# Thirty small loads on SP's queue, and 384 skipped products at the head of TensorE's program, in a decode kernel that streams a key and value cache

## The chip, the cores and the metric

One core of one Trainium2 chip runs the whole kernel. The metric is the time of one execution on the device, in microseconds (us); the figure for a kernel is the median of several runs.

## The reference, cut to what matters

One decode step for two batch entries. A token vector `x` (2 x 512) is normalised, projected to 32 query heads, and attends over a cache of 32,768 keys and values for each of 8 key/value heads. A small two-layer network on the same normalised vector gives a gate.

```python
xn = _layernorm(A_x)
q  = (xn @ wq)                                   # 512 x 4096
scores = einsum("bhqd,bhkd->bhqk", q, k) * 128**-0.5
o  = einsum("bhqk,bhkd->bhqd", softmax(scores), v)
s  = o.reshape(2, 1, 4096) @ wo                  # 4096 x 512
h  = relu(xn @ w1 + b1) ** 2
g  = silu(h @ w2 + b2)
out = A_x + s * g
```

The caches are `k_cache` and `v_cache`, each 2 x 8 x 32768 x 128 in float32. They make up almost all of the bytes that are read.

## The kernel before, in words

**Tiles.** There are 16 steps, one for each pair of batch entry and key/value head. The keys of a step come in two loads (`load_k`) of 128 partitions x 16,384 numbers into `kring`, which has three slots of 64 rows; its values come in two loads of the same size (`load_v`) into `vbuf`. Each such load is 8.4 MB. VectorE transposes the keys in blocks (`dve_keys`, L309), TensorE makes scores from them (`te_scores`, L270) and weights the values (`te_values`, L280), ScalarE evicts and exponentiates.

**Order of the loads.** All large loads are issued by SP through the helper `load` (L84), one after another, in the order in which the program writes them. A load into `kring` waits for VectorE's transposes of what stood there (`transposed`); a load into `vbuf` waits for TensorE's products with the values that stood there (`PV`). While SP waits for one mark, everything behind it on its queue waits too. ACT issues four small loads at the start and the store of the result at the end.

**Start.** SP issues the query weights `wq` into `vbuf` (L138), then the first keys (L139) and one half load of the next (L140). `wq_in` releases the projection products (L210), whose result is turned into `qT` by copies and transposes (L227 to L235). The first instructions of TensorE are four transposes of the normalised vector (L200); they wait for VectorE.

**Middle.** From the second step on, PE, ScalarE and VectorE each run a hardware loop (L442 to L489), whose outermost PE loop is placed at slot 0 of a block of its code (`head_slot`, L442). SP's loads are written out (L495 to L502).

**End.** The last two value loads go into `kring` and `vbuf` (L507, L508), then the output weights `wo` in five pieces (L515 to L519). The last products are L525 and L533; `spare` (L538 to L540) adds products whose result nobody reads. The result leaves by ACT's store (L587).

Of the kernel before, what the change touches and what calls it, by code (L numbers as in the profile page):

```python
# [5 lines left out]
F32 = mybir.dt.float32  # L6
# [5 lines left out]
P = 128  # L12
# [40 lines left out]
def gqa_decode_kernel(nc, x, kc, vc, wq, wo, w1, b1, w2, b2, out):  # L53
    B, _, D = x.shape
    _, HKV, SK, DH = kc.shape
# [15 lines left out]
    def sb(name, *shape):  # L71
        return nc.alloc_sbuf_tensor(name, (P,) + shape, F32).ap()

    def bank(name, n=1):
        t = nc.alloc_psum_tensor(name, (P, n * 512), F32).ap()
        return t if n == 1 else t.rearrange("p (n f) -> p n f", n=n)

    SP, ACT, DVE, POOL, TE = (Lane(nc, e, n) for e, n in (
        (nc.sync, "sp"), (nc.scalar, "act"), (nc.vector, "dve"), (nc.gpsimd, "pool"), (nc.tensor, "pe")))
    tensor, vector, scalar, gpsimd, sync = nc.tensor, nc.vector, nc.scalar, nc.gpsimd, nc.sync  # L80

    def load(lane, dst, src, sem, *marks):
        lane.wait(*marks)
        return sem.after(lane.eng.dma_start(dst, src))  # L84

    def dma(name):
        return Count(nc, name, 16)
# [9 lines left out]
    def k_rows(m):  # L97
        s, u = divmod(m, 2)
        return rows(kc, s).rearrange("(p u r) d -> p u r d", p=P, u=2)[:, u]
# [20 lines left out]
    def transposed(q):  # L120
        return KT[1].at(q + 1)

    def load_k_half(m, i, *marks):
        c = k_order(m)[i][1]
        return load(SP, k_slot(2 * m + i), k_rows(m)[:, c * SLOT:(c + 1) * SLOT], k_sems[m % 2], *marks)

    def load_k(m):
        a = m % 2
        return load(SP, kring[:, a * SLOT:(a + 2) * SLOT, :], k_rows(m), k_sems[a], transposed(max(2 * m - 2, -1)))
# [6 lines left out]
    wo_t = [kflat[:, a * SLOT * DH:a * SLOT * DH + 16 * D].rearrange("p (r e) -> p r e", r=16) for a in (2, 0)]  # L136

    wq_in = load(SP, wq_t, wq.rearrange("(p d) f -> p d f", p=P), dma("wq"))  # L138
    k0_in = load_k(0)  # L139
    load_k_half(1, 1)  # L140

# [8 lines left out]
    ident = sb("ident", P)  # L150
# [21 lines left out]
    mx_ps, fin_ps, pj_ps, acc_ps = bank("mx_ps"), bank("fin_ps"), bank("pj_ps"), bank("acc_ps")  # L172
# [22 lines left out]
    t = DVE(lambda: vector.reciprocal(st[:, 3:4], st[:, 2:3]), t)  # L195
    t = DVE(lambda: vector.tensor_scalar(xn, xn, st[:, 3:4], None, op0=ALU.mult), t)
    xnT = sb("xnT", ND, 32)
    TE.wait(t, have_ident)
    for d in range(ND):
        t = TE(lambda: tensor.transpose(mx_ps[:, d * P:(d + 1) * P], xn.rearrange("p (k d) -> p d k", d=ND)[:, d], ident))  # L200
# [22 lines left out]
    for f in range(2):  # L223
        for h in range(REP):
# [8 lines left out]
            v = t_ps.rearrange("p (e g y) -> p g e y", e=4, g=NG)  # L233
# [10 lines left out]
    def set_q(s):  # L244
        hkv, b = divmod(s, B)
        return POOL(lambda: gpsimd.tensor_tensor(
            qz.rearrange("p e (x h) -> p e x h", h=REP),
            qT[:, b, hkv].rearrange("p h e -> p e h")[:, :, None, :].to_broadcast([P, 4, 8, REP]),
            bm[:, None, :, None].to_broadcast([P, 4, 8, REP]), op=ALU.mult),
            *((have_qT, have_bm) if s == 0 else (PA[1].at(4 * s + 1),)), on=QZ if s else None)  # L250
# [125 lines left out]
    for d in range(ND):  # L376
        for g in range(NG):
            t = TE(lambda: tensor.matmul(pj_ps[32 * g:32 * g + 32, :FG], xnT[:, d, :], w1_t[:, d, g * FG:(g + 1) * FG],
                                         start=False, stop=(d == ND - 1)))
# [37 lines left out]
    for j in range(4):  # L417
        t = TE(lambda: tensor.matmul(fin_ps[32 * j:32 * j + 32, 0:P], ones[0:1, 0:32], b2t[:, j * P:(j + 1) * P],
                                     start=False, stop=True, skip_group_check=True))
# [12 lines left out]
    act_probs(0, have_p)  # L432


    def registers(eng, **values):
        for name, v in values.items():
            r = eng.alloc_register(name)
            eng.reg_mov(r, v)
            yield r

    rq, rv, rs = registers(tensor, rq=5, rv=16, rs=1)
    with nc.Fori(1, NS, 1, engines=[PE], head_slot={PE: 0}):  # L442
        with nc.Fori(0, 2, 1, engines=[PE]):
# [13 lines left out]
        tensor.reg_add(rs, rs, 1)  # L457

    aq, av, as_ = registers(scalar, aq=6, av=1, as_=1)
    with nc.Fori(1, NS, 1, engines=[AE]):  # L460
        for u in range(2):
# [10 lines left out]

    seen = Count(nc, "seen").sem
    dq, dk, ds = registers(vector, dq=5, dk=48, ds=1)
    with nc.Fori(1, NS, 1, engines=[VE]):
        for q in range(4):
# [18 lines left out]
    for s in range(1, NS):  # L495
# [5 lines left out]
        if s + 1 < NS:  # L501
            set_q(s + 1)  # L502


    L = NH - 2
    va, vb = dma("va"), dma("vb")
# [3 lines left out]
    wo_in = {}  # L510
# [27 lines left out]
    def spare(n):  # L538
        for _ in range(n):
            tensor.matmul(pj_ps[:, 0:P], ident, ident, start=True, stop=True)  # L540
# [33 lines left out]
    t = columns4(31, 32)  # L574

    spare(4)
    SP.wait(wo_in[31])
    idle = Count(nc, "idle")
    for _ in range(4):
        idle.after(sync.nop())  # L580
# [35 lines left out]
```

## Time and profile before

| | us |
|---|---|
| runs: median of 3 | 1303.49 |
| runs: lowest, highest | 1303.37, 1303.68 |
| profiled execution: span from first to last instruction | 1302.6 |
| PE busy in it | 639.7 |
| DVE busy in it | 619.0 |
| share of 16 DMA engines that SP's queue (q1) kept busy | 99.6% |

Of the profiled execution only the span is recorded, and no time of its own beside it; the median of the runs is 0.9 us above that span. Busy times of engines overlap one another and do not add up to the span. The share of the DMA engines is the time that packets took, over 16 engines and the whole span. q1 is SP's queue, q10 is ACT's; q8 and q14 bring instructions.

### The profile page before, as it was taken

What the parts mean: (1) busy time and instruction counts of PE and PEld (TensorE: products, weight loads), DVE (VectorE), ACT (ScalarE), POOL (GpSimd) and SP (SyncE); (2) the same over time, 40 slices, a digit from 0 to 9 for tenths busy, and PEclk for the clock granted to TensorE, in tenths of its full rate; (3) what the DMA queues carried; (4) which work ended last, traced back from release to release, by engine and by line L of the source; (5) the groups of instructions that cost most, each with busy time, mean ns of one, the idle gap of its engine ahead of it and who ended that gap; (6) DMA issues with size and microseconds to landing.
All of it is one profiled execution on the core that took longest, in us unless ns stands there. A gap on an engine that the chain in (4) does not pass through costs nothing.

```text
span 1302.6 us, 10806 instructions
## 1 busy us (share of the span) xinstructions
PE 639.7 (49%) x4710; PEld 175.6 (13%) x4710; DVE 619.0 (48%) x305; ACT 128.6 (10%) x262; POOL 11.9 (1%) x41
## 2 busy tenths in 40 slices
PE   3555444555535455544536543444653444554368
PEld 1111110111101011110101111111110111111014
DVE  2565553436555344655435555343655534455410
ACT  0111011111001011000111101011100101101010
POOL 0000000000000000000000000000000000000000
PEclk9778677878767787777788777678877778877789
DMA  9999999999999999999999999999999999999998
GB/s 419 418 448 423 441 427 435 431 437 433 431 437 427 443 427 441 429 441 427 439 427 437 433 431 437 427 443 427 441 429 441 427 439 427 439 431 429 441 425 356
DMA packets 10703, 561.14 MB, mean 431 GB/s; under 512 B 1199, under 2 KB 1219, under 8 KB 1478
## 3 DMA queue, kind: packets, MB, share of 16 engines
q1 hardware_dynamic: 10656, 560.99, 99.6%
q8 instruction: 6, 0.10, 0.0%
q10 hardware_dynamic: 38, 0.02, 0.0%
q14 instruction: 3, 0.02, 0.0%
HBM read 561.01 MB, written 0.00 MB: 431 GB/s over the span
## 4 chain that ended last, share of the span: by engine, by line
DMA 77%; DVE 12%; issue 10%; PE 1%; SPq 0%; DVEq 0%
DMA kring<-in_A_k_cache 73%; DVE kt L309 12%; DMA kring<-in_A_v_cache 2%; DMA kring<-in_A_wo 2%; PE o_ps L280 1%; PE acc_ps L533 0%; PE pj_ps L540 0%; SPq L84 0%; DVEq L308 0%; PE acc_ps L411 0%
## 5 line engine op out<-in xcount | busy, mean ns | idle before, releaser
L309 DVE STREAM_TRANSPOSE kt<-kring 128x4096 f32<-128x4096 f32 x128 | 557.6, 4414 | 449.4 <-DMA kring<-in_A_k_cache 449.4
L270 PE MATMUL ps_s<-kt,qz 128*32 128x512 f32 x2048 | 333.5, 779 | 603.4 <-DVE kt L309 603.4
L280 PE MATMUL o_ps<-vbuf,pTh 128*16 128x512 f32 x1984 | 227.5, 612 | 1.8 <-DMA vbuf<-in_A_v_cache 1.8
L270 PEld LDWEIGHTS ps_s<-kt,qz 128*32 128x32 f32 x2048 | 67.8, 128 | 845.1 <-issue 669.9
L333 ACT ACTIVATE sc<-ps_s,halves 128x512 f32<-128x512 f32 x64 | 46.6, 729 | 866.5 <-PE ps_s L270 866.5
L280 PEld LDWEIGHTS o_ps<-vbuf,pTh 128*16 128x16 f32 x1984 | 57.8, 101 | 178.0 <-issue 158.6
L343 ACT COPY pTh<-pT_ps 64x256 f32<-64x256 f32 x128 | 46.9, 366 | 39.6 <-PE pT_ps L299 21.6
L315 DVE CUSTOM_DVE_ANT_0 sc<-sc 128x1024 f32<-128x1024 f32 x16 | 19.6, 1225 | 54.9 <-ACT sc L333 54.9
L318 DVE CUSTOM_DVE_ANT_0 junk<-mx_ps,other 128x128 f32<-128x128 f32 x16 | 4.7, 292 | 82.1 <-PE mx_ps L288 82.1
L336 ACT ACTIVATE sc<-sc,nm 128x1024 f32<-128x1024 f32 x16 | 18.4, 1149 | 108.9 <-DVE nm L318 108.9
L328 DVE TENSOR_REDUCE hr<-fin_ps 128x4 f32<-128x64 f32 x16 | 3.6, 225 | 48.5 <-PE fin_ps L292 48.5
L292 PE MATMUL fin_ps<-ident,o_sb 128*128 128x128 f32 x64 | 10.5, 286 | 17.4 <-DVE o_sb L485 17.2
L348 ACT COPY o_sb<-o_ps 128x512 f32<-128x512 f32 x15 | 8.8, 586 | 97.2 <-PE o_ps L280 97.2
L299 PE MATMUL pT_ps<-ident,sc 128*128 128x128 f32 x128 | 17.5, 282 | 0.0
L299 PEld LDWEIGHTS pT_ps<-ident,sc 128*128 128x128 f32 x128 | 15.3, 147 | 0.0
L280 PE MATMUL o_ps<-kring,pTh 128*16 128x512 f32 x64 | 9.3, 749 | 9.0 <-DMA kring<-in_A_v_cache 9.0
L493 POOL COPY oT<-ho 128x4 f32<-128x4 f32 x15 | 2.8, 188 | 1147.2 <-DVE ho L329 1147.2
L210 PE MATMUL pT_ps<-vbuf,xnT 128*32 128x512 f32 x64 | 8.5, 693 | 7.4 <-DMA vbuf<-in_A_wq 7.4
L227 DVE COPY kt<-pT_ps 128x512 f32<-128x512 f32 x8 | 5.0, 683 | 13.2 <-PE pT_ps L210 13.2
L540 PE MATMUL pj_ps<-ident 128*128 128x128 f32 x88 | 10.8, 278 | 0.0
L540 PEld LDWEIGHTS pj_ps<-ident 128*128 128x128 f32 x88 | 10.1, 192 | 1.9 <-issue 1.9
L485 DVE TENSOR_TENSOR o_sb<-o_sb,o_ps 128x512 f32<-128x512 f32 x15 | 10.2, 682 | 0.0
(90 smaller groups left out, 105.5 us busy)
## 6 DMA issues: line engine op xcount, KB each, us to landing
kring<-in_A_k_cache SPq DMA_DIRECT2D x4, 4096.0 KB, 23.8
vbuf<-in_B_w SPq DMA_DIRECT2D x2, 3584.0 KB, 28.5
kring<-in_A_wo SPq DMA_DIRECT2D x1, 4096.0 KB, 41.2
kring<-in_A_wo SPq DMA_DIRECT2D x1, 2304.0 KB, 25.5
kring<-in_A_wo SPq DMA_DIRECT2D x1, 1024.0 KB, 27.6
kring<-in_A_wo SPq DMA_DIRECT2D x1, 512.0 KB, 28.4
vbuf<-in_A_v_cache SPq DMA_DIRECT2D x31, 30.1
kring<-in_A_k_cache SPq DMA_DIRECT2D x30, 29.8
```

Of the source, the lines that this page charges most:

```text
L270: i = tensor.matmul(ps_s[32 * g:32 * g + 32, :], qz[:, 2 * y + e, :], kt[y][:, g * NO:(g + 1) * NO, 32 * e:32 * e + 32], start=(y == 0 and ...
L280: mm_ = tensor.matmul(o_ps[32 * g:32 * g + 16, :], pTh[:, 2 * g + c, 2 * i:2 * i + 2, :, :].rearrange("p o y h -> p (o y h)"), vt[:, lo:lo ...
L292: t = tensor.transpose(fin_ps[:, i * P:(i + 1) * P], o_sb[:, i * DH:(i + 1) * DH], ident)
L299: t = tensor.transpose(pT_ps[:, k // 4, (k % 4) * P:(k % 4 + 1) * P], p[:, k * P:(k + 1) * P], ident)
L309: KT[y].after(vector.transpose(kt[y], k_slot(q)[:, :, 64 * y:64 * y + 64]))
L315: return DVE(lambda: vector.tensor_tensor_reduce(scf[0], scf[0], scf[1], 1.0, -3.4e38, ALU.add, ALU.max, rm), mark, on=on)
L333: ACT(lambda: scalar.mul(sc[c][:, :, :, u], ps_s.rearrange("p (o w) -> p o w", w=32), halves[:, c:c + 1]), *marks, on=EV)
L336: return ACT(lambda: scalar.activation(scf[0], scf[0], AF.Exp, bias=nm, scale=SCALE, accum_out=l), mark, on=on)
L343: i = scalar.copy(pTh[64 * a:64 * a + 64, :, :, y, :], v[64 * y:64 * y + 64, :, :, a0, a, :])
L348: scalar.copy(o_sb, o_ps).then_inc(OE.sem, 32)
L485: DVE(lambda: vector.tensor_add(o_sb, o_sb, o_ps), on=OSR)
L540: tensor.matmul(pj_ps[:, 0:P], ident, ident, start=True, stop=True)
```

## The change

It has three parts.

1. Behind `wq` and ahead of the first keys, SP issues 15 loads of 1, 2, ... 15 rows of 16 numbers (64 B) each from `w2` into a new tile `steps`, on a semaphore `stairs0`. Nothing computes with `steps`.
2. The same 15 loads stand a second time, on `stairs1`, behind the last value load of the middle and ahead of the last two value loads. Each waits for `stairs0`. SP's wait at the end (L580 before) takes `stairs1` in too.
3. Ahead of TensorE's first transposes stands a block of 6 x 64 = 384 products of `ident` with itself into `pj_ps`, within a branch that runs only if a register differs from 0. The register is set to 0, so that TensorE jumps over them. The helper `registers` moves up for that; its other uses stay.

```diff
@@ -136,6 +136,14 @@
     wq_in = load(SP, wq_t, wq.rearrange("(p d) f -> p d f", p=P), dma("wq"))
+    steps = nc.alloc_sbuf_tensor("steps", (15, 15, 16), F32).ap()
+
+    def stairs(sem, *marks):
+        for k in range(1, 16):
+            have = load(SP, steps[0:k, k - 1, :], w2[0:k, 16 * k:16 * k + 16], sem, *marks)
+        return have
+
+    first_stairs = stairs(dma("stairs0"))
     k0_in = load_k(0)
@@ -195,6 +203,16 @@
     xnT = sb("xnT", ND, 32)
...
+    (skip,) = registers(tensor, skip=0)
+    with tensor.If_ne(skip, 0):
+        for _ in range(6 * 64):
+            tensor.matmul(pj_ps[:, 0:P], ident, ident, start=True, stop=True)
     TE.wait(t, have_ident)
@@ -502,6 +514,8 @@
+    last_stairs = stairs(dma("stairs1"), first_stairs)
+
     L = NH - 2
@@ -574,7 +588,7 @@
-    SP.wait(wo_in[31])
+    SP.wait(wo_in[31], last_stairs)
```

SP's queue at its start, before: the query weights, the first keys, half a load of the next, the first-layer weights.

```order
L84 DMA vbuf<-in_A_wq 128x16384 [waits barrier_Pool_Activation_PE_DVE_SP_release]
L84 DMA kring<-in_A_k_cache 128x16384
L84 DMA kring<-in_A_k_cache 128x8192
L84 DMA vbuf<-in_B_w 128x7168 [waits pe]
L84 DMA kring<-in_A_k_cache 128x8192 [waits kt_1]
```

The same place with the change, from the 13th small load on; `steps` is the new tile, `in_B_w` here the array `w2`.

```order
L84 DMA steps<-in_B_w 13x16
L84 DMA steps<-in_B_w 14x16
L84 DMA steps<-in_B_w 15x16
L84 DMA kring<-in_A_k_cache 128x16384
L84 DMA kring<-in_A_k_cache 128x8192
L84 DMA vbuf<-in_B_w 128x7168 [waits pe]
```

Fifteen issues now stand between the query weights and the first keys; none of them waits for anything.

SP's queue near its end with the change; before, the three `steps` rows and the twelve like them ahead are not there, and the two value loads follow straight on the loads of the middle.

```order
L84 DMA steps<-in_B_w 13x16 [waits stairs0]
L84 DMA steps<-in_B_w 14x16 [waits stairs0]
L84 DMA steps<-in_B_w 15x16 [waits stairs0]
L84 DMA kring<-in_A_v_cache 128x16384 [waits kt_1]
L84 DMA vbuf<-in_A_v_cache 128x16384 [waits pv]
L84 DMA kring<-in_A_wo 128x8192 [waits kt_1]
```

The small loads stand ahead of a load that waits for VectorE's transposes (`kt_1`).

TensorE's program at its head, with the change; before, it begins with the row of `mx_ps<-ident,kt` (L200 there).

```order
L213 COMPARE_AND_BRANCH
L215 MATMUL pj_ps<-ident 128x128 x384
L213 UNCONDITIONAL_BRANCH
L218 MATMUL mx_ps<-ident,kt 128x128 x4
L228 MATMUL pT_ps<-vbuf,xnT 32x512 x32
```

Everything behind the branch stands 384 products further down in the program; its order is the same.

## Rows read from the trace of the kernel before

**Rows 1.** The page: span, and busy time by engine.
```profile
span 1302.6 us, 10806 instructions
PE 639.7 (49%) x4710; PEld 175.6 (13%) x4710; DVE 619.0 (48%) x305; ACT 128.6 (10%) x262; POOL 11.9 (1%) x41
```
**Rows 2.** The page: DMA queues: packets, MB, share of 16 engines over the span.
```profile
q1 hardware_dynamic: 10656, 560.99, 99.6%
q8 instruction: 6, 0.10, 0.0%
```
**Rows 3.** Chain of waits from 1180 us: start us, us, what.
```profile
1191.73 29.81 DMA kring<-in_A_k_cache
...
1230.44 29.81 DMA kring<-in_A_v_cache
...
1270.06 27.60 DMA kring<-in_A_wo
...
1297.70 1.08 PE acc_ps L533 x32
```
**Rows 4.** DMA from 1297 to 1303 us: busy tenths in 40 slices; q1's share.
```profile
DMA  7655443332210000000400000100000000000000
...
q1 hardware_dynamic: 132, 0.30, 12.8%
```
**Rows 5.** Timeline of SP's queue, 0 to 110 and from 1200 us: start, us, engine, line.
```profile
0.74 0.38 SPq L84 DMA_DIRECT2D vbuf<-in_A_wq  x1
1.17 0.90 SPq L84 DMA_DIRECT2D kring<-in_A_k_cache  x2
...
1209.36 0.33 SPq L84 DMA_DIRECT2D vbuf<-in_A_v_cache  x1
1230.44 0.33 SPq L84 DMA_DIRECT2D kring<-in_A_v_cache  x1
```
**Rows 6.** Line L84: issues of ACT's queue, ns min/median/max, first and last start us.
```profile
L84 ACTq DMA_DIRECT2D kt<-in_A_x x1: 1221/1221/1221, 1.4 to 1.4; - x1
L84 ACTq DMA_DIRECT2D b1t<-in_B_b x1: 304/304/304, 2.7 to 2.7; - x1
```
**Rows 7.** DMA from 1302.06 to 1302.20 us, the store of the result.
```profile
DMA packets 12, 0.00 MB, mean 29 GB/s; under 512 B 4, under 2 KB 12, under 8 KB 12
...
q10 hardware_dynamic: 12, 0.00, 12.1%
```
**Rows 8.** Timeline of ACT's queue near the end: start, us.
```profile
1300.79 0.63 ACTq L587 DMA_DIRECT2D out<-fin  x1
```
**Rows 9.** DMA queue q8 in 38:41, 101:104 and 1264:1268 us: packets, MB, share.
```profile
q8 instruction: 1, 0.02, 1.9%
...
q8 instruction: 1, 0.02, 2.2%
...
q8 instruction: 1, 0.02, 1.7%
```
**Rows 10.** DMA from 104 to 1264 us, where q8 has no line.
```profile
q1 hardware_dynamic: 8636, 503.06, 100.2%
```
**Rows 11.** DMA issues in 1205:1215 us: the value load, us to landing.
```profile
vbuf<-in_A_v_cache SPq DMA_DIRECT2D x1, 31.5
```
**Rows 12.** Tile vbuf from 1240 to 1290 us: the value load issued at 1248.1.
```profile
DMA to landing us min/median/max: 31.5/31.5/31.5
```
**Rows 13.** Timeline of PE at the start, in brackets the idle time before.
```profile
14.39 1.13 PE L200 MATMUL mx_ps<-ident,kt 128*128 128x128 f32 x4 [14.39 <-DVE kt L196]
22.90 8.52 PE L210 MATMUL pT_ps<-vbuf,xnT 128*32 128x512 f32 x64 [7.38 <-DMA vbuf<-in_A_wq]
```
**Rows 14.** Timeline of DVE at the first keys.
```profile
43.30 17.43 DVE L309 STREAM_TRANSPOSE kt<-kring 128x4096 f32<-128x4096 f32 x4 [9.26 <-DMA kring<-in_A_k_cache]
```
**Rows 15.** The page: groups of L540: busy, mean ns of one, idle before.
```profile
L540 PE MATMUL pj_ps<-ident 128*128 128x128 f32 x88 | 10.8, 278 | 0.0
L540 PEld LDWEIGHTS pj_ps<-ident 128*128 128x128 f32 x88 | 10.1, 192 | 1.9 <-issue 1.9
```

More of the change, by code (lines that the diff above doesn't have):

```diff
@@ L197, in gqa_decode_kernel, with registers @@
     xnT = sb("xnT", ND, 32)
+    def registers(eng, **values):
+        for name, v in values.items():
+            r = eng.alloc_register(name)
+            eng.reg_mov(r, v)
+            yield r
+    (skip,) = registers(tensor, skip=0)
+    with tensor.If_ne(skip, 0):
+        for _ in range(6 * 64):
+            tensor.matmul(pj_ps[:, 0:P], ident, ident, start=True, stop=True)
     TE.wait(t, have_ident)
@@ L432, in gqa_decode_kernel @@
     act_probs(0, have_p)
[L435 to L439, printed above, removed]
     rq, rv, rs = registers(tensor, rq=5, rv=16, rs=1)
```

## The prediction

> **What bounds the kernel now.** I began with the page's span and busy times [rows 1] beside its DMA queues [rows 2]. PE and DVE are each busy for about half of the 1302.6 us; SP's queue keeps the 16 DMA engines busy for 99.6% of it. So the reader should look at the transfers first, and ask of any added work whether it lengthens them. The chain of waits [rows 3] says the same: from one large load's issue to that of the next but one, from 1191.73 to 1230.44, pass 38.71 us for two loads, 19.36 us each, and the chain's steps are loads, with short products only behind the last one. From 104 to 1264 us the same queue has the engines at 100.2% [rows 10], that is, without a hole. The end is read from the last six microseconds of DMA [rows 4]: the busy share falls from 7 tenths at 1297 us to nothing in the 14th slice of 0.15 us, at 1299.1. The 16 engines do not end together, and the slowest one sets the end.
>
> From this comes the rule of the sum. Engine time that is added counts only if it lies on the DMA engine that ends last, or if a queue runs dry. What PE, SP or DVE do beside it counts only if it holds up the issue of a load until no earlier load is left to transfer.
>
> **The small loads: transfer time.** A set has 1 + 2 + ... + 15 = 120 rows of 64 B. The trace has no 64 B row. The nearest is the store of the result [rows 7]: 12 packets, 8 of them rows of 512 B and 4 below that, took 12.1% of 16 engines in 0.14 us, 0.27 us of engine time, or 0.023 us a packet. That is 1.9 engines busy on average within the store, with 4 endings, so such a transfer spreads over several engines. I take a load of k rows as one row and one ending on each of k engines; then an engine gets at most 15 pairs a set, and 30 in all. At 0.045 us a pair that is 1.35 us for the busiest engine, which is the upper end, since its rows have eight times the bytes. The lower end is 0: the engine so loaded may be one that ends early. A gain is left to the levelling below. Averaged over 16 engines a set gives 7.5 pairs each, 15 in both, 0.7 us at 0.045; I take **+0.4 us**, near the lower half, because the rows are shorter than those measured.
>
> **The small loads: SP's time.** Issues of loads of few rows, on ACT's queue, took 0.30 us (four rows) and 1.22 us (two rows, the first one) [rows 6]. Fifteen take 4.6 to 18.3 us. In the first set they hold back the first keys, which were issued at 1.17 us [rows 5] and would then go out at 5.7 to 19.4. The cover is the transfer of the query weights: PE waits for them until 22.90 [rows 13], so the engines have work till then even at the upper bound. In the second set SP is free at 1209.69, and the next large load goes out at 1230.44, when its mark comes [rows 5]; 1209.69 + 18.3 is 1228.0. Cost **0**. If an issue took over 1.4 us, SP would be late and the difference would be paid in full. Queued behind the second set are the last two value loads and `wo`, which PE waits for; their marks come later than SP does. The extra wait on `stairs1` ends before that on `wo`, which was issued after it.
>
> **The skipped products.** 44 products of L540 show up as 88 MATMULs and 88 weight loads [rows 15], so 384 products are 1,536 instructions that TensorE jumps over. Executed, they would take 768 x 0.278 = 213 us; the register is 0, so they are not. What can be paid is code loading. Queue q8 brought 6 packets, 0.10 MB [rows 2], each about 1 us of one engine: 1.9% of 16 engines over 3 us is 0.91, 2.2% of 3 us is 1.06, 1.7% of 4 us is 1.09; I use 1.07 [rows 9]. They come behind 38 and 101 us, while PE works through the code ahead of the loop, none from 104 to 1264 while it loops [rows 10], and again behind 1264. So code comes as PE advances to it, not all at once. By the listing the program before has 385 products for these 6 packets, about 64 for each; the skipped 384 are some six packets' worth.
>
> How many more packets are loaded? Between 0 (the jump finds its target) and 6 (all that is jumped over comes too). I take 2: the packet in which the jump lands, and the one behind it, since neither can have been at hand from the reading order that rows 9 and 10 show. Their cost in engine time is 2 x 1.07 = 2.1 us. On the path it is 2.1 only if both fall on the engine that ends last. One load shows how a packet hides: the value load issued at 1209.36 landed after 31.5 us [rows 11], the one issued at 1248.06 landed after 31.5 us as well [rows 12], although a packet of q8 ran between 1264 and 1268 us [rows 9], while it was under way. That packet's engine had slack. I take **0**, with +2.1 as the upper end.
>
> The other end is a gain: packets now meet other engines, and the ends may draw level. In the last stretch q1 is busy for 12.8% of 16 engines in 6 us [rows 4], 12.3 engine-us or 0.77 us for each engine, so level engines would end at 1297.8 in place of 1299.1. The gain is **at most 1.3 us**.
>
> For PE itself the jump may end in a wait for code. The cover: its first transposes start at 14.39 and then it idles 7.38 us for the query weights [rows 13]. Code that arrives by 20 us costs nothing. The added register write, comparison and branch go by in that time too.
>
> **Sum.** 0.4 + 0 + 0 + 0 = +0.4 us. Of the profiled execution only the span is known, 1302.6 us, which becomes 1303.0; the runs' median lies 0.9 us above, so I add to the median: 1303.49 + 0.4 = **1303.9 us**. About 0.2%, 2.6 us, is what a measurement of this kernel can tell from no change. This forecast lies within it, from 1302.2 (levelled, loads free: -1.3) to 1306.0 (both code packets on the last engine: 2.1 + 0.4).
>
> **Rivals.**
>
> *Code packets pile up on one engine (slower).* If the queue q8 always used one engine and that one ended last, each extra packet would cost its 1.07 us: with 6 extra, 6.4 + 0.4 = 6.8, **1310.3 us**. It decides from the third packet on (3 x 1.07 = 3.2 us, over 2.6). Against it: the packet behind 1264 us did not move the load in flight [rows 11, 12]. For it: nothing in these views names the engine. Chance 0.08.
>
> *The code is late (slower).* The target arrives behind the query weights and first keys, which fill the engines' queues from the start. By 20 us it is free. Later than that, PE's products and the copies behind them shift, and the next cover is VectorE's 9.26 us of idle time ahead of the first keys' transposes at 43.30 [rows 14]; so it decides from about 29 us on. If the code came only behind the first keys, at 43 us, the lack would be 14 us: 1303.9 + 14 = **1317.9 us** if loads already queued covered none of it. Against it: the packets of rows 9 come well ahead of need. The Trainium skill, "Runtime: NRT & Kernel Launch", section on instruction fetch mechanics, says that a taken branch out of the loaded window breaks the sequential prefetch and stalls for the target page; no row of before shows such a jump. Chance 0.03.
>
> *The small loads run one after another (slower).* From the issue of the result's store at 1300.79 [rows 8] to the end of the span pass 1.8 us. If each small load held the queue so long, 30 x 1.8 = 54 us, **1357 us**; it decides from 0.09 us a load. Against it: 99.6% busy with over 70 large loads in a row on that queue [rows 2] leaves 0.4%, 5.2 us, for all their endings together. The Trainium skill, "DMA: Bandwidth & Descriptors", anatomy of one DMA, gives a fixed cost of about 2.0 us for each transfer on GpSimd's path; paid one by one it would make +60 us. Chance 0.02.
>
> *A gain beyond levelling (faster).* Engines that step out of phase could each pass their rows faster. At 19.36 us a load there are some 66 such loads' worth of bytes; 0.04 us less in each would make 2.6 us, **1300.9 us**. Nothing in the rows shows that the pace depends on phase. Chance 0.03.
>
> *The change does nothing.* If the small loads and the jump cost no engine on the path anything, the time stays at 1303.5, inside the forecast.
>
> **How the numbers follow.** Forecast and "does nothing" together 0.84, rivals 0.08 + 0.03 + 0.02 + 0.03. The range 1302.2 to 1306.0 leaves out the rivals' 0.16. Faster by over 0.2%: 0.03; within: 0.84; slower: 0.08 + 0.03 + 0.02 = 0.13.
>
> **What would show it.** Right: q1 still near 99.6%; 240 more short rows and their endings on q1; a large load still 19.36 us behind the one before; 8 packets on q8, two of them before 22 us; L210 still released by the query weights near 23 us; the next value load issued within 0.5 us of 1230.4; the last DMA slice near 1299. Wrong: idle slices of DMA around 22 us or 1230 us (SP's issues), PE's first transposes after 20 us (late code), 10 or more packets on q8 with an end past 1302 us (pile-up), or holes of a microsecond behind each small load.

## The result, and the profile after

The changed kernel takes 1306.61 us (median of 11 runs, 1306.39 to 1307.04), the kernel before 1303.66 us on the same chip (11 runs, 1303.37 to 1303.74): **2.95 us slower**, a ratio of 1.0023 with an interval of 1.0015 to 1.0031. It lies outside the range of the prediction, 1302.2 to 1306.0, and just past the 0.2% that was called "no change". The span of the profiled execution grew by 2.4 us, from 1302.6 to 1305.0; the rest, about half a microsecond, is not in the spans of these two executions. Of the kernels below, the kernel before among them, a few executions took 1382 to 3165 us; without these no median given here moves by more than 0.04 us.

The page of the changed kernel: the span and the queues that answer to [rows 1, 2].

```profile
span 1305.0 us, 10840 instructions
q1 hardware_dynamic: 11136, 561.01, 99.6%
q8 instruction: 8, 0.13, 0.0%
```

q1 has 480 packets more, the 240 short rows and their 240 endings; q8 has the 8 packets that were forecast, in place of 6. The engines' busy share is the same 99.6%. The loss therefore does not show as idle engine time: it lies in time in which packets count as under way. Whether the small packets take it or the large ones have become longer, this view does not tell; the packets themselves are read further below.

Where the time enters is seen on SP's queue. Its timeline in the changed kernel, at the start and from 1200 us on (start us, us, engine, line), answers to [rows 5].

```profile
0.74 0.38 SPq L84 DMA_DIRECT2D vbuf<-in_A_wq  x1
1.17 5.55 SPq L84 DMA_DIRECT2D steps<-in_B_w  x15
6.76 0.87 SPq L84 DMA_DIRECT2D kring<-in_A_k_cache  x2
...
1210.70 0.33 SPq L84 DMA_DIRECT2D vbuf<-in_A_v_cache  x1
1211.07 5.24 SPq L84 DMA_DIRECT2D steps<-in_B_w  x15
1231.79 0.35 SPq L84 DMA_DIRECT2D kring<-in_A_v_cache  x1
1249.43 0.35 SPq L84 DMA_DIRECT2D vbuf<-in_A_v_cache  x1
```

Fifteen issues took 5.55 and 5.24 us, and SP was idle again at 1216.3, more than 15 us before the next mark: issue time was covered, as forecast. But the first of the last two value loads goes out at 1231.79, where it went out at 1230.44 [rows 5]: 1.35 us have been lost before the second set is transferred. The second part shows in that load's way to its landing (tile `kring`, 1215 to 1245 us, changed kernel):

```profile
DMA to landing us min/median/max: 31.3/31.3/31.3
```

Before, it took 29.8 us [rows 3]. So 1.35 us at its issue and 1.5 us on its way make 2.85 us, close to the 2.95 measured. This one load, the first large one behind the second set, serves below as the gauge: the delay of its issue tells what was lost up to the second set, the delay of its landing what the second set adds. The chain of waits from 1180 us on (start us, us, what) shows that the pace between the sets did not change and how the delay reaches the end:

```profile
1154.39 29.80 DMA kring<-in_A_k_cache
...
1193.08 29.81 DMA kring<-in_A_k_cache
...
1249.43 33.04 DMA vbuf<-in_A_v_cache
...
1282.51 8.80 PE o_ps L298 x64
...
1294.72 5.36 PE pj_ps L539 x48
...
1302.48 1.09 PE pj_ps L554 x8
```

Two large loads still take 38.69 us (1154.39 to 1193.08). The last value load lands 33.04 us after its issue; before it was 31.5 [rows 12]. Its products and what depends on them follow it, later than `wo` this time: the chain has no `wo` step, where [rows 3] had one of 27.60 us. The two ends lie close together: with the same loads and no skipped products (`e1_both_sets` below) the chain goes through `wo` again.

The skipped products did what was forecast of them. PE's timeline at the start, to be read beside [rows 13]:

```profile
14.32 1.13 PE L218 MATMUL mx_ps<-ident,kt 128*128 128x128 f32 x4 [14.32 <-DVE kt L204]
24.32 8.47 PE L228 MATMUL pT_ps<-vbuf,xnT 128*32 128x512 f32 x64 [8.87 <-DMA vbuf<-in_A_wq]
```

The transposes wait for VectorE and start as early as before; code is not late. The query weights land 1.4 us later, at 24.32.

### The profile page after: what moved, and what is told of

It is laid out like the page before. It is cut to its first block, busy times and chain, and to the rows that moved or that the text cites. A ratio compares the mean times of both kernels' runs of the same rounds, so it can differ in the third digit from the quotient of the medians.

```text
span 1305.0 us, 10840 instructions
## 1 busy us (share of the span) xinstructions
PE 638.8 (49%) x4710; PEld 175.7 (13%) x4710; DVE 619.0 (47%) x305; ACT 128.5 (10%) x262; POOL 11.9 (1%) x41
## 3 DMA queue, kind: packets, MB, share of 16 engines
q1 hardware_dynamic: 11136, 561.01, 99.6%
## 4 chain that ended last, share of the span: by engine, by line
DMA 75%; DVE 12%; issue 10%; PE 2%; SPq 0%; ACT 0%; DVEq 0%
DMA kring<-in_A_k_cache 72%; DVE kt L327 12%; DMA vbuf<-in_A_v_cache 3%; PE o_ps L298 1%; PE pj_ps L539 0%; SPq L84 0%; PE acc_ps L547 0%; PE ps_s L288 0%; PE pj_ps L554 0%; DVEq L326 0%; PE mx_ps L576 0%; PE fin_ps L310 0%; ACT o_sb L564 0%; DVE om L572 0%; ACT oR L577 0%
## 5 line engine op out<-in xcount | busy, mean ns | idle before, releaser
L228 PE MATMUL pT_ps<-vbuf,xnT 128*32 128x512 f32 x64 | 8.5, 689 | 8.9 <-DMA vbuf<-in_A_wq 8.9
## 6 DMA issues: line engine op xcount, KB each, us to landing
kring<-in_A_k_cache SPq DMA_DIRECT2D x30, 29.8
```

## The experiments

Each kernel ran in turns with the kernel before on the same chip; its medians there were 1303.58 to 1303.73 us. The interval of a ratio reaches 0.0008 to 0.0013 either way, 1.0 to 1.7 us, so that a difference of less is not clear of noise by the times alone; the profiles are read beside them. Theory R in the first batch is that a run of small rows makes an engine late, theory C that the extra code packets do. The later ones are named in the expectations. All kernels but `e2_skip_only` leave out the skipped products and their branch.

### One part alone

`e1_both_sets`: both sets, the branch and its products left out.

```diff
-    (skip,) = registers(tensor, skip=0)
-    with tensor.If_ne(skip, 0):
-        for _ in range(6 * 64):
-            tensor.matmul(pj_ps[:, 0:P], ident, ident, start=True, stop=True)
```

> Both sets of small loads, without the skipped products. Theory R (runs of small rows make an engine late; the engines with the most rows end last): nearly all of the change's +2.95 us, 1305.7 to 1306.6. Theory C (the two extra code packets set the end): at most +0.5 us, 1303.6 to 1304.2. If the two share it: near 1305.

Measured: 1306.64 us, **+3.04**, ratio 1.0024 (1.0014 to 1.0033). The whole of the change's loss is there without the products.

`e2_skip_only`: the branch and its products, neither set of loads.

```diff
-    first_stairs = stairs(dma("stairs0"))
...
-    last_stairs = stairs(dma("stairs1"), first_stairs)
...
-    SP.wait(wo_in[31], last_stairs)
+    SP.wait(wo_in[31])
```

> The skipped products alone. Theory R: 1303.6 to 1304.3, with 8 code packets on q8 as in the change and the value load of the end issued within 0.5 us of 1230.4. Theory C: 1305.5 to 1306.6, with that issue near 1231.8 as in the change.

Measured: 1303.62 us, **+0.02**, ratio 1.0000 (0.9991 to 1.0009). Its page and its chain of waits:

```profile
q8 instruction: 8, 0.13, 0.0%
```
```profile
1230.54 29.81 DMA kring<-in_A_v_cache
```

The 8 code packets are there, and the gauge is at 1230.54 and 29.81, where [rows 3] has 1230.44 and 29.81. In this kernel too the query weights came late, PE's timeline says:

```profile
24.19 6.07 PE L220 MATMUL pT_ps<-vbuf,xnT 128*32 128x512 f32 x28 [8.76 <-DMA vbuf<-in_A_wq]
```

With the loads and without the products, in `e1_both_sets`, they come at 22.96. So the 1.3 us there go with the skipped products, two code packets more in the trace, and cost nothing at the end. Theory C falls.

`e3_first_set` and `e4_second_set`: one set each.

```diff
-    last_stairs = stairs(dma("stairs1"), first_stairs)
...
-    SP.wait(wo_in[31], last_stairs)
+    SP.wait(wo_in[31], first_stairs)
```

> The first set alone (its mark is waited for at the end). Theory R: half of what both sets cost, 1304.5 to 1305.2, and the value load that was issued at 1230.44 goes out 1 to 1.4 us later. Theory C: no change, 1303.4 to 1304.0.

```diff
-    first_stairs = stairs(dma("stairs0"))
...
-    last_stairs = stairs(dma("stairs1"), first_stairs)
+    last_stairs = stairs(dma("stairs1"))
```

> The second set alone. Theory R: the other half, 1304.5 to 1305.2, with the issues up to 1230.44 where they were and the last value load landing 1 to 1.5 us later than 31.5 us after its issue. Theory C: no change, 1303.4 to 1304.0.

Measured: first set 1304.94 us, **+1.34**, ratio 1.0010 (1.0001 to 1.0019); second set 1304.58 us, **+0.98**, ratio 1.0008 (0.9999 to 1.0016). The interval of the second just takes in no change; its gauge does not. Chain of waits, first set alone:

```profile
1232.17 29.81 DMA kring<-in_A_v_cache
```

and second set alone:

```profile
1230.43 30.97 DMA kring<-in_A_v_cache
```

The first set moves the issue and not the way to the landing, the second the way to the landing and not the issue. The issue came 1.73 us late, where 1 to 1.4 was expected. With the second set alone the lateness is on the way of the gauge, 30.97 in place of 29.81, and not of the last value load, which the expectation named and which took 31.1 us there. By the medians the two add to 2.32 us, short of the 3.04 of both, but within the intervals; by the gauge they make 1.73 + 1.16 = 2.89, and `e1_both_sets` has 2.99 there (1231.67 and 31.57). Whether anything is missing is not shown. A reason that would fit: the engines do not end together [rows 4], so the first microsecond that an engine loses can in part be its slack.

### What of a set costs

`e5_even` and `e11_even15`: the same number of rows on every engine, 8 or 15 a set.

```diff
-        for k in range(1, 16):
-            have = load(SP, steps[0:k, k - 1, :], w2[0:k, 16 * k:16 * k + 16], sem, *marks)
+        for k in range(8):
+            have = load(SP, steps[:, k, :], w2[0:16, 16 * k:16 * k + 16], sem, *marks)
```

`e11_even15` has `range(15)` there. In these kernels and the next ones the tile `steps` has the size that the loads need.

> Both sets as 8 loads of 16 rows of 64 B each (128 rows a set in place of 120), so that every engine gets 8 rows a set. Theory L (only the unequal share hurts; level work costs its engine time of about 0.02 us a row and ending): 1303.7 to 1304.1. Theory R (a run of small rows makes the large packet behind it late on every engine that gets one): about 1 us a set for 8 rows, by half of what 15 cost, 1305.0 to 1306.0.

> Each set as 15 loads of 16 rows of 64 B: every engine gets the run that only the busiest got in the change. Theory E (many small loads in a run, each with its ending, hold an engine up, and more than in proportion to the shortest runs): 8 loads cost 0.81 us a set, so 15 cost 1.5 us a set in proportion or up to 2 us: 1306.8 to 1307.9. If the run's cost were a fixed sum from some length on: 1305.2 as with 8.

Measured: 8 loads 1305.21 us, **+1.62**, ratio 1.0012 (1.0003 to 1.0021); 15 loads 1308.10 us, **+4.52**, ratio 1.0034 (1.0021 to 1.0046), 0.2 us above the range of theory E. Level shares do not help: theory L falls. The gauge in the chain of waits, with 8 loads:

```profile
1231.40 30.66 DMA kring<-in_A_v_cache
```

and with 15:

```profile
1232.85 32.04 DMA kring<-in_A_v_cache
```

With 15 loads it is 2.41 us late at its issue and 2.23 us later still at its landing, 4.64 us for 4.52 measured. A set costs 0.81 us with 8 loads and 2.26 us with 15, so each of the last seven costs (2.26 - 0.81) / 7 = **0.21 us**. By this estimate 0.81 us pays for about four of the eight, and the other four come free.

`e6_five`: the first five loads of each set.

```diff
-        for k in range(1, 16):
+        for k in range(1, 6):
```

> Both sets cut to their first 5 loads, 1 to 5 rows, so that no engine gets more than 5 rows in a run. Theory F (each row costs the same, so 5 of 15 cost a third): +1.0 us, 1304.4 to 1304.9. Theory R with a threshold (the first few rows of a run hide behind the transfer in flight): +0.0 to +0.4 us, 1303.6 to 1304.0.

Measured: 1303.68 us, **+0.09**, ratio 1.0000 (0.9991 to 1.0009). The gauge is back where it was:

```profile
1230.43 29.80 DMA kring<-in_A_v_cache
```

The first five loads cost nothing that shows, and theory F falls.

`e7_spread`: the same 30 loads, each behind a large one but for the last three, which stand together; the second tile half keeps the two loads of a size apart.

```diff
+    stairs = dma("stairs0")
+    def stair(i):
+        k, o = 1 + i // 2, 16 * (i % 2)
+        return load(SP, steps[o:o + k, k - 1, :], w2[0:k, 16 * k:16 * k + 16], stairs)
...
     for s in range(1, NS):
         for m in (2 * s, 2 * s + 1):
...
+            last_stairs = stair(m - 2)
```

> The same 30 loads, one behind each large value load of the loop in place of two runs of 15 (the last three stand together), so that the busiest engine still gets 30 rows. Theory F (each row costs the same wherever it stands): 1306.2 to 1306.9. Theory R (only a run costs): 1303.6 to 1304.3.

Measured: 1303.83 us, **+0.24**, ratio 1.0001 (0.9992 to 1.0010), with all 240 rows and endings still on q1:

```profile
q1 hardware_dynamic: 11136, 561.01, 99.6%
```

The loads cost by standing in a long run, not by their number.

`e8_rows_512B`: rows of 512 B.

```diff
-            have = load(SP, steps[0:k, k - 1, :], w2[0:k, 16 * k:16 * k + 16], sem, *marks)
+            have = load(SP, steps[16 * (k % 8):16 * (k % 8) + k, k // 8, :], w2[0:k, 0:P], sem, *marks)
```

> Both sets with rows of 512 B in place of 64 B, on partitions spread over the tile; numbers of loads and rows as in the change. Theory R (a row costs by being a row): +3.0 to +3.7 us, 1306.6 to 1307.3. Theory B (rows are slow because they are under 512 B): +0.3 to +1.2 us, 1303.9 to 1304.8.

Measured: 1306.73 us, **+3.14**, ratio 1.0024 (1.0014 to 1.0033). Eight times the bytes, on other partitions, change nothing: theory B falls, and that the rows are small is not the cost.

`e9_one_load` and `e12_three_loads`: 15 rows for every engine, in one load or in three.

```diff
-        for k in range(1, 16):
-            have = load(SP, steps[0:k, k - 1, :], w2[0:k, 16 * k:16 * k + 16], sem, *marks)
-        return have
+        return load(SP, steps, w2[0:16, 0:480].rearrange("p (j e) -> p j e", j=15)[:, :, 0:16], sem, *marks)
```

`e12_three_loads` takes the same rows five at a time:

```diff
-        for k in range(1, 16):
-            have = load(SP, steps[0:k, k - 1, :], w2[0:k, 16 * k:16 * k + 16], sem, *marks)
+        for k in range(0, 15, 5):
+            have = load(SP, steps[:, k:k + 5, :], w2[0:16, 0:480].rearrange("p (j e) -> p j e", j=15)[:, k:k + 5, 0:16], sem, *marks)
```

> Each set as one load of 16 partitions x 15 rows of 64 B: every engine gets a run of 15 rows, as the busiest did in the change, but one ending in place of 15. Theory E (the endings between the rows make the run slow): 1303.6 to 1304.2. Theory R (rows in a run are slow, endings or not): the even loads' +1.62 us for 8 rows an engine becomes 3 us or more, 1306.4 to 1308.0.

> Each set as 3 loads of 16 partitions x 5 rows of 64 B: 15 rows for every engine in a run, with 3 endings. Theory E with the first few endings hidden: as the one load, 1304.0 to 1304.5. If the rows between endings matter: over 1304.8.

Measured: one load 1304.22 us, **+0.49**, ratio 1.0004 (0.9995 to 1.0013); three loads 1304.28 us, **+0.70**, ratio 1.0005 (0.9996 to 1.0014). That is against +4.52 for the same rows in 15 loads. The gauge with one load:

```profile
1230.64 30.08 DMA kring<-in_A_v_cache
```

So rows in a run are cheap, 0.25 us a set for 15 of them on each engine, and it is the 15 separate loads, each with an ending on each of its engines, that hold the engines up. Whether the ending or the start of the next load does it was not separated: each load has one of either.

Where the lost time lies can be read from the packets. The first set passes in the stretch from 16 to 30 us. Queue q1 there (packets, MB, share of 16 engines), in the kernel before, in `e11_even15` (15 loads) and in `e9_one_load`:

```profile
q1 hardware_dynamic: 112, 6.29, 103.7%
```
```profile
q1 hardware_dynamic: 576, 5.26, 103.1%
```
```profile
q1 hardware_dynamic: 368, 6.31, 105.6%
```

In the same time at nearly the same share, 15 loads let a sixth fewer bytes through, and one load none fewer. Shorter windows part the packets; the view counts a packet whole in the window in which it begins, so that a share can exceed 100% (the next large packets of `e11_even15` stand from 26.25 us on). Three windows of 0.05 us: one large packet of the kernel before (22.15 to 22.2 us), eight small ones of `e11_even15` (22.5 to 22.55) and a large one right behind them (22.6 to 22.65):

```profile
q1 hardware_dynamic: 1, 0.07, 304.4%
```
```profile
q1 hardware_dynamic: 8, 0.00, 10.0%
```
```profile
q1 hardware_dynamic: 1, 0.07, 545.2%
```

304.4% of 16 engines over 0.05 us is 2.43 us. The small packets took 0.010 us each. The large packet behind the run took 4.36 us, and on the 16 engines 4.1 to 4.8. With 8 loads these packets took 2.9 to 3.5 us, with one load 2.5, with the first five loads 2.42 but for two engines (2.49 and 2.86), and in the change from 2.42 to 4.67, since there the engines get unequal numbers of rows. For `e11_even15` that is 2.0 us for the large packet and 0.3 us for 30 small ones, 2.3 us for each engine, against the 2.26 us that a set costs. So the rows and endings themselves take little; the first large packet behind the run, on each engine, is what becomes longer. What inside it waits, no view shows.

`e10_act_queue`: the loads of both sets issued by ACT, the second behind its loop.

```diff
-            have = load(SP, steps[0:k, k - 1, :], w2[0:k, 16 * k:16 * k + 16], sem, *marks)
+            have = load(ACT, steps[0:k, k - 1, :], w2[0:k, 16 * k:16 * k + 16], sem, *marks)
...
-    first_stairs = stairs(dma("stairs0"))
...
     biases_in = load(ACT, x4[0:P:Y, :], x2.rearrange("b (j e) -> j b e", j=ND), biases, zero_x4)
+    first_stairs = stairs(dma("stairs0"))
```

> The same two sets issued by ACT on its own queue, the first behind ACT's four loads, the second behind its loop. Theory Q (a run is slow only as a run on one queue; on another queue the rows go between SP's large packets one at a time): 1303.6 to 1304.4. Theory R without that: +2 to +3 us, 1305.6 to 1306.6.

Measured: 1303.74 us, **+0.01**, ratio 1.0001 (0.9991 to 1.0010). Its page has the packets on ACT's queue, q10:

```profile
q1 hardware_dynamic: 10656, 560.99, 99.6%
...
q10 hardware_dynamic: 518, 0.04, 0.0%
```

The same 30 loads, each in a run as ACT issues them, cost nothing there. ACT issued the second set at 1251 to 1257 us, some 40 us later than SP did, so that set met other large loads; the first set stood at the start as before. From 16 to 30 us:

```profile
q1 hardware_dynamic: 112, 6.29, 103.7%
q10 hardware_dynamic: 91, 0.01, 0.5%
```

SP's queue has the very line of the kernel before, so no large packet became longer there. ACT had issued the first set by 9.6 us, and its packets go on passing until past 64 us: they lie strewn among the large packets, which fits the expectation. The sentence of the Trainium skill, "DMA: Bandwidth & Descriptors", on issuing engines, that a second queue saves only issue time, does not hold for this run, for small loads beside a queue that is never empty: 3.04 us against 0.01.

No version here beats the kernel before; the best ones tie with it.

## Why the prediction was wrong, point by point

- **The term that failed: the transfer time of the small loads.** It was taken as +0.4 us, with 1.35 us as the upper end, and measured +3.04. The price of 0.045 us for a row with its ending came from the store of the result [rows 7]. That store is one load's worth: no large packet came behind it. It prices rows and endings, and these are cheap indeed, 0.02 us a pair in `e11_even15`, but it says nothing of what fifteen loads in a row do to the packet behind them. The sum has no term for that packet, and it is where the time lies: 4.1 to 4.8 us in place of 2.42 behind 15 loads, about 0.21 us for each load past the first four, five times the price taken. What makes that packet wait stays open.
- **The rival that came nearest was written off.** "The small loads run one after another" named the mechanism in outline and its point of decision, 0.09 us a load. Its price, 1.8 us a load, was about nine times too high; the measured 3.04 us are 0.10 a load over all thirty, just past that point. The argument against it was that some 70 large loads end on the queue with only 0.4% of idle time [rows 2]; but those endings stand 19.36 us apart, and where the small loads stood apart as well, in `e7_spread`, they cost 0.24 us in all. The 2.0 us that the Trainium skill, "DMA: Bandwidth & Descriptors", anatomy of one DMA, gives for a transfer on GpSimd's path are not paid one by one either: no run came near 60 us.
- **Its sign in the profile was wrong as well.** Holes behind each small load were to show it. q1 stays at 99.6 or 99.7% in every kernel: the lost time lies within large packets that count as busy, and the gauge load or the packets behind a run show it.
- **Busiest engine, half right.** By the prediction's rule the engine with most rows sets the time. In the first set of the change the engine that lost most lost about 2.5 us (2.25 on the large packet, 0.3 on its small ones), the average engine 0.9 (from the packets between 16 and 30 us), and the gauge was 1.35 us late, between the two. Filling up the others to 15 rows costs 1.5 us more (4.52 against 3.04).
- **The range.** Its upper end, 1306.0, adds the code packets' 2.1 us to the 0.4 and leaves out the 1.35 that the prediction itself names as the upper end of the small loads. With it the range would have reached 1306.9 and held the result, but by luck: the code packets, most of that distance, cost nothing.
- **SP's time, right.** 5.55 and 5.24 us for fifteen issues, within 4.6 to 18.3, and covered both times.
- **The skipped products, right.** Two packets more on q8, no late code, +0.02 us in all (`e2_skip_only`). That the query weights land 1.3 to 1.4 us later with them was not foreseen, and costs nothing.
- **Signs that were forecast.** The value load "within 0.5 us of 1230.4" failed, at 1231.79, and that was the sign to look for; the last loads end at 1301.5, where 1299 was forecast; pace of the large loads, packet counts and the release of L228 (L210 before) by the query weights held.

## What to carry to other kernels

On a queue that streams large loads without a hole, a few small loads between two large ones cost nothing that these runs could tell, but a run of them with rows on every engine delayed the stream by about 0.2 us for each load past the fourth or so, and rows of 64 and of 512 B cost alike. Gather small pieces into one load with many rows, strew the loads between large ones, or issue them from another queue. The busy share of the DMA engines does not show this loss; the time from issue to landing of the next large load does, and so does the time of the packets behind the run.

## What the runs showed that was not expected

- Fifteen loads of 16 rows of 64 B, 15 KB in all, delayed the stream by 2.26 us a set, and the same rows as one load by 0.25 us. The small packets took 0.010 us each; the large packet behind them took up to 4.8 us in place of 2.42.
- Rows of 512 B cost as much as rows of 64 B in the same loads, +3.14 against +3.04 us. The Trainium skill, "DMA: Bandwidth & Descriptors", specifications, names 512 B as the least size for full rate; in these runs the size made no difference, the number of loads did.
- With two code packets more, of 1.0 to 1.9 us each, the query weights landed 1.3 us later, and 1.2 ms on nothing of it was left in the time.
